# The last block's output tiles stored in two transfers of 64 rows each, three of the eight issued by ScalarE, under another instruction order

## The chip, the cores and the metric

The kernel runs on one core of one Trainium2 chip. The metric is the device time of one execution in microseconds (us). Three runs of the kernel before gave 1031.87, 1032.00 and 1032.98 us, a median of 1032.0 us.

## The reference

The program computes an attention with random features and feeds its output to a two-layer network with a softplus between the layers. What is computed, cut to the core:

```python
q_s, k_s = q / D**0.25, k / D**0.25              # batch 8, heads 8, seq 576, head_dim 64
def phi(x):                                      # 128 features
    h = x @ omega.T - sum(x * x) / 2
    return exp(h - max(h)) / sqrt(128)
kv, z = phi(k_s).T @ v, sum(phi(k_s))            # per batch and head
x = (phi(q_s) @ kv) / (phi(q_s) @ z + 1e-6)      # as 4608 tokens x 512
h = x @ w_in                                     # 512 x 2048
g = max(h, 0) + log1p(exp(-abs(h)))
out = g @ w_out                                  # 2048 x 512, all in float32
```

## The kernel before

The 4608 tokens are worked off as nine blocks of 512. Eight blocks hold the first 512 tokens of each batch; the ninth, called the last block here, holds the 64 tokens left over in each of the eight batches. For each block the network runs in 16 steps. A step is layer 1 for 128 of the 2048 hidden columns (12 matmuls into the PSUM tile `h`, lines 933 to 935), the softplus (three ScalarE activations at lines 939, 942 and 945, one VectorE operation at 948), a split of the result `u` into a rounded high part `gh` (line 952) and a rest `gl` (line 956), and layer 2 (12 matmuls into the four accumulators `acc`, lines 962 to 964, three for each 128 tokens). There are two buffers of each of `u`, `gh` and `gl`. Step 15 of block 8 is written (8,15) here, and so in the tile names of an order (`h_8_15`).

The attention work of the following batch is woven between the steps: projections of keys and queries (`ppk`, `ppq`, line 400, or line 425 from the split tiles `spk`, `spq` that lines 414 and 418 make), sums over keys (`kt`, line 564), and the product that gives `x` (`xp`, line 875). It ends at about 830 us; after that only the network of the last blocks is left.

No engine's order is written out by hand. Every piece of work is an object with an engine, an estimated cost, a due time, predecessors and buffers; `in_order` is a list scheduler that walks a modelled clock and takes, among the pieces that could start soonest, the one with the earliest due time. Some hundred constants (due times, `AHEAD`, `PATIENCE`, `GLUE`, `SPREAD`) decide that order, and the order of the DMA issues on SyncE's queue with it. All DMAs are issued by SyncE (SP).

After step 15 of a block, each of its four accumulators (`tt` 0 to 3) is copied to an output tile `o`, left half by VectorE (`left`, line 996) and right half by ScalarE (`right`, line 999), and stored (`store`). For the first eight blocks the store writes 128 consecutive rows of 2 KB (line 1004). In the last block a tile's 128 rows belong to two batches, 64 rows each; the store writes them in one transfer whose output side has the form 2 x 64 x 512 (line 1006).

Of the kernel before, what the change touches and what calls it, by code (L numbers as in the profile page):

```python
# [20 lines left out]
S = 576  # L21
D = 64
# [12 lines left out]
AHEAD = 312.45  # L35
MARGIN = 0.00
START = {"SP": 0.75, "ACT": 1.9, "PE": 4.6}
SLOW = 10.94
FILL = 0.3
DENSE = 12  # L40
PATIENCE = {"PE": 0.00, "DVE": 0.02, "ACT": 0.17, "POOL": 15.27, "SP": 4.12}
LEAN = {"DVE": 0.56, "POOL": 0.00, "ACT": 0.00}
SPREAD = ((0, 10.51), (17, 8.16))
# [4 lines left out]
GLUE = 67.48  # L48
HOLD = 0.09
START_PACE = 5.26  # L50
EARLY_Q = 7.20
# [135 lines left out]
def favor_softplus_kernel(ctx, tc, q0, k0, qx, kx, tx, vv, om, wi, wo, out):  # L187
# [78 lines left out]
    def plan_weights(nm, fc, due):  # L266
# [36 lines left out]
        def low_part(e):  # L303
# [5 lines left out]
            "SP", 1.46, due + 31.61, load, delay=DL, spare=0 if last else 2,  # L309
# [38 lines left out]
    def plan_unit(q, kind, us, due, early, other=None):  # L348
# [115 lines left out]
        def exponent(j):  # L464
# [9 lines left out]
            "SP", dma(size), due + 15.20, load, behind=prev.get("load"),  # L474
# [7 lines left out]
        if q.b < SPLIT["t" if tail else kind]:  # L482
            r = do("DVE", dve(w), due + 10.58, norms, after=[s], behind=prev.get("norms"), take=sm)
            prev["norms"] = r
            p = do(
                "PE", 0.02 + 0.224 * nt, due - 96.65, project, after=[ld], mode="r",
# [5 lines left out]
            for j in range(2):  # L492
                e = do(
                    "DVE", dve(n // 2 * M), due - 36.44, lambda j=j: maxima(j), after=[p, e], give=[(b, "x")] if j and not early else [],
                )
            e = do("DVE", dve(n), due - 37.34, less_norms, after=[e], port=True)
            e = do("DVE", dve(n), due - 45.13, bias, after=[e], port=True)
            for j in range(2):
                give = [(b, ("ppb", j))]
                es.append(do(  # L500
                    "ACT", n // 2 * 0.25, due - 0.03, lambda j=j: exponent(j), after=[e], behind=es[0] if j else None,
                    give=give + ([(b, "sms")] if j else []),
                ))
        else:
            hs, ls, l = [], [], None
            for j in range(2):
                h = do(
                    ("ACT", "DVE"), (act(w) + 0.1, dve(w, 2) + 0.115), due - 4.01, lambda e, j=j: high(e, j), after=[ld], behind=hs[-1] if hs else None,
                    take=[] if j else [("sp", b, "sps")], port=True,
                )  # L510
                hs.append(h)
                l = do(("DVE", "POOL"), (dve(w) + 0.115, pool(w) + 0.2), due - 76.28, lambda e, j=j: low(e, j), after=[h], behind=l, port=True)
                ls.append(l)
            r = do("DVE", dve(w), due + 30.96, norms, after=[s] + ls, behind=prev.get("norms"), take=sm, give=[(b, "x")])
            prev["norms"] = r
            e, p = None, prev.get("product")
            for t in range(nt):
                p = do(
                    "PE", 0.236, due - 9.84, lambda t=t: product(t), after=ls, behind=p, take=[(kind_, b, ("ppb", t))],
                    give=[(b, "sps")] if t == nt - 1 else [],  # L520
                )
                c = do(
                    ("ACT", "DVE"), (act(2 * M, PSUM), dve(2 * M)), due - 86.17, lambda e, t=t: first(e, t), after=[p], behind=e,
                    take=[] if t else phs,
                )
                e = do("DVE", dve(2 * M), due - 13.53, lambda t=t: second(t), after=[c], give=[(b, ("ppb", t))])
            prev["product"] = p
            e = do("DVE", dve(n * M) + 0.07 * (len(to) - 1), due + 196.21, all_maxima, after=[e, r])
            e = do("DVE", dve(n), due - 55.07, less_norms, after=[e], port=True)
            e = do("DVE", dve(n), due - 36.67, bias, after=[e], port=True)  # L530
            es = []
            for t in range(nt):
                es.append(do(
                    "ACT", 0.587, due - 50.02, lambda t=t: exponents(t), after=[e], behind=es[-1] if es else None,
# [11 lines left out]
        for i in range(len(us)):  # L546
            done.append(plan_queries(q, us[i], due + 1.81 * i, b, es, f"{nm}_{i}", 4 * i))
        plan_flip(q, us, due + 48.99 * (len(us) - 1), b, nm, done)

    def plan_keys(q, us, due, b, es, early):  # L550
# [36 lines left out]
        def plan_turn(after, give=[]):  # L587
            old = quads[q.n - 2].nums if q.n >= 2 else []
            t = do("PE", 0.15, due - 81.14, turn, after=[after], take=[(any_, q.slots, "kv")], give=give)
            q.kvl = do(  # L590
                ("ACT", "DVE"), (act(2 * M, PSUM), dve(2 * M)), due + 3.70, turned, after=[t] + old,
# [4 lines left out]
        if early:  # L596
# [16 lines left out]
            def first_scaled():  # L613
# [4 lines left out]
                "PE", 0.97 if u < 4 else 0.5, due + 9.14, outer, after=es + [q.kvm], give=[(b, "x")],  # L618
                take=[("acc", q.slots, "kt")] if u == 0 else [],
            )  # L620
            if u == 4:
                q.kvl = do(
                    "ACT", act(4 * D + 4, PSUM), due - 59.41, first_scaled, after=[q.kvm], give=[(q.slots, "kt")],
# [4 lines left out]
        def add(e):  # L628
# [16 lines left out]
            ("POOL", "DVE"), (k * pool(w), k * dve(w) + 0.2), due - 71.26, add, after=es + [q.sum],  # L645
# [35 lines left out]
        def in_z():  # L681
# [6 lines left out]
        ldv = do("SP", 1.8, due + 66.39, load_v, take=[("v", q.slots, "v")], delay=DL)  # L688
        q.kvm = do(
            "PE", 0.1 + 0.224 * 10, due - 74.27, burst, after=q.es + [ldv, q.sum], take=[(any_, q.slots, "kt")],  # L690
# [3 lines left out]
            "DVE", dve(4 * M), due - 33.63, flip_sums, after=[q.sum], take=[("flip", q.slots, "st"), ("few", q.slots, "few")], port=True,  # L694
        )
        a = do("ACT", act(2 * M, PSUM), due - 46.64, lambda: scaled(2 * M), after=[q.kvm, z], give=[(q.slots, "kt")])
        plan_turn(a, [(q.slots, "s")])
        z = do("DVE", dve(4 * M), due + 5.39, sums, after=[z], give=[(q.slots, "st")])
        z = do("DVE", 0.55, due - 98.77, last_sums, after=[z], port=True)
        r = do("SP", 0.55, due - 30.52, out_z, after=[z], give=[(q.slots, "few")], delay=DL)  # L700
        q.zc = do("SP", 0.73, due + 123.44, in_z, after=[r], take=[("zb", q.slots, "zb")], delay=DL)

    def plan_first(q, u, due, b, es, nm):
# [51 lines left out]
        def x_low():  # L755
# [3 lines left out]
        t = do("PE", 0.13 * n, due - 118.52, turn, after=es, take=[("any", y, "tp")])  # L759
        h = do(("ACT", "DVE"), (act(n * M, PSUM), dve(n * M)), due - 116.63, turned, after=[t], give=[(y, "tp")])  # L760
        a = do(
            "PE", 0.9, due - 165.51, num, after=[h, q.kvl], take=[("any", y, "nb")], behind=q.nums[-1] if q.nums else None,
            give=[(q.slots, "zb")] if u == NU - 1 else [],
        )
        i = do("DVE", 0.285, due - 134.25, invert, after=[a], take=[("dn", y, "dns")], port=True)
        v = do("DVE", dve(4 * D), due - 140.10, divide, after=[i], give=[(y, "nb"), (y, "dns")])
        k = do("PE", 0.28, due - 64.26, back, after=[v], take=[("any", y, "xb")], give=[(b, "x")])
        q.nums.append(a)
        h = do(
            ("DVE", "ACT"), (dve(2 * w), act(2 * w, PSUM)), due + 2.16, x_high, after=[k], take=[("pt", y, "rs")] if u == 4 else [],  # L770
# [5 lines left out]
        l = do("DVE", dve(2 * w), due + 7.12, x_low, after=[h], give=[(y, "xb")])  # L776
# [3 lines left out]
    def plan_queries(q, u, due, bu, es, nm, first):  # L780
# [21 lines left out]
        def divide(e):  # L802
# [4 lines left out]
            "DVE", 1.6 if u < 4 else 1.35, due + 60.18, den, after=es + [q.zc], take=[("dn", b, "dns")],  # L807
            give=[(q.slots, "zb")] if u == NU - 1 else [], port=True,
        )
        d = do("DVE", 0.09, due - 79.51, invert, after=[d])  # L810
        return do(("POOL", "DVE"), (1.0 * f, dve(n * M)), due + 169.04, divide, after=[d], give=[(b, "dns")], port=True)

    def plan_flip(q, us, due, bu, nm, done):
# [25 lines left out]
        def back():  # L839
# [12 lines left out]
            "DVE", dve(n * M), due + 20.79, flip, after=done, give=[(bu, "phs")], take=[("flip", b, "vs")], port=True,  # L852
        )
        o = do("SP", 0.6 * n_out, due + 53.49, away, after=[t], give=[(b, "vs")], delay=DL, take=[("fd" if u < 4 else "ft", b, "ds")])
        h = do(
            "SP", 0.6 * n_in, due + 4.59, back, after=[o], delay=DL, behind=prev.get("turn"),
# [8 lines left out]
    def plan_x(q, due, t0, w, any_, qt):  # L865
# [27 lines left out]
        def x_low(p):  # L893
# [4 lines left out]
            "PE", 0.00342 * w + 0.02, due - 27.71, num, after=qt["works"] + [q.kvl],  # L898
# [24 lines left out]
    def plan_step(i, t0, n, fc, due, acc, box):  # L923
# [50 lines left out]
        s = do("ACT", act(n, PSUM), due - 35.05, magnitude, after=[a], take=[("u", b, "us")])  # L974
        s = do("ACT", act(n), due + 24.62, decay, after=[s])
        s = do("ACT", act(n), due - 82.94, log, after=[s])
        p = do("DVE", dve(n), due - 23.55, plus, after=[s], give=[(b, "hs")])
        h = do(("DVE", "ACT"), (dve(n, 2), act(n)), due + 23.89, high, after=[p], take=[("g", b, "gs")], port=True)
        l = do(("DVE", "POOL"), (dve(n), pool(n)), due + 31.26, low, after=[h], give=[(b, "us")], port=True)
        box["l1"], ends = a, []  # L980
        for tt in range(n // P):
            e = do(
                "PE", 0.692, due + 10.38, lambda tt=tt: layer2(tt), after=[l, done_w["o", fc]], behind=box.get("l2"),
# [7 lines left out]
        for tt in range(n // P):  # L991
# [9 lines left out]
            def store(tt=tt, o=o):  # L1001
# [216 lines left out]
```

## Time and profile before

| | us |
|---|---|
| median of the runs | 1032.0 |
| the profiled execution's own time | 1030.81 |
| its span, first to last instruction | 1029.0 |
| TensorE busy in the span | 990.7 (96%) |
| mean granted TensorE clock | 0.987 of full speed |

Busy time is the time in which an engine has an instruction of the program at work. The span is what the trace covers; the 1.8 us between it and the execution's own time lie around it. A time such as 1004.03 is counted from the first instruction of the span.

### The profile page before, as it was taken

Reading aid. Unit: us, or ns where it says so; the run is one execution under the profiler, and the core shown is the slowest. Engines: PE = TensorE matmul, PEld = TensorE weight load, DVE = VectorE, ACT = ScalarE, POOL = GpSimd, SP = SyncE. Lnnn points to the kernel's source line nnn. Section 1 sums busy time; section 2 is a strip of 40 time slices with the busy share of each in tenths; the row PEclk is TensorE's granted clock in tenths of the full one; section 3 lists DMA queues with packets and bytes.
Section 4 is the critical chain, followed back from the end, with each engine's and each line's share of the span. In section 5 each row is a group of like instructions: output and inputs, shape, how many; then the busy total and the mean of one; then the engine's idle time right before and its main releaser. Section 6 shows DMA issues by size and latency. Waiting matters only on the chain.

```text
span 1029.0 us, 16459 instructions
## 1 busy us (share of the span) xinstructions
PE 990.7 (96%) x5436; PEld 791.2 (77%) x5436; DVE 713.0 (69%) x1860; ACT 684.5 (67%) x1638; POOL 240.3 (23%) x235
## 2 busy tenths in 40 slices
PE   9999998999999999999999999999999999999990
PEld 8777676787878777777787878878777788888880
DVE  7999998878777877788688868787788342222220
ACT  6999885867676767776786668676767454444440
POOL 2143442242323232322321322323223000000000
PEclk9999998999999999999999999999999999999996
DMA  9874345433333333433434243334331210001001
GB/s 349 312 275 158 123 129 165 138 101 121 113 117 101 130 110 88 134 103 90 132 113 146 75 131 132 126 96 124 118 89 55 83 62 1 1 1 40 1 1 41
DMA packets 64445, 113.78 MB, mean 111 GB/s; under 512 B 18536, under 2 KB 37096, under 8 KB 64360
## 3 DMA queue, kind: packets, MB, share of 16 engines
q1 hardware_dynamic: 64360, 112.73, 34.0%
q8 instruction: 43, 0.70, 0.3%
q14 instruction: 42, 0.34, 0.1%
HBM read 85.68 MB, written 27.03 MB: 110 GB/s over the span
## 4 chain that ended last, share of the span: by engine, by line
PE 76%; DVE 10%; ACT 5%; DMA 4%; issue 2%; POOL 0%; SPq 0%; DVEq 0%; ACTq 0%
PE acc L962 11%; PE h L933 11%; PE h L934 11%; PE h L935 11%; PE acc L963 11%; PE acc L964 11%; PE kt L564 3%; PE ppk L400 3%; PE xp L875 2%; PE ppq L425 2%; DVE junk L795 2%; DMA xq<-q 1%; DMA xq<-qx 1%; DVE flq L826 1%; DVE u L948 1%
## 5 line engine op out<-in xcount | busy, mean ns | idle before, releaser
L962 PE MATMUL acc<-wo,gh 128*128 128x512 f32 x576 | 231.4, 402 | 4.4 <-ACT gh L952 4.4
L933 PE MATMUL h<-xh,wi 128*128 128x512 f32 x576 | 228.2, 396 | 0.0
L963 PE MATMUL acc<-wo,gh 128*128 128x512 f32 x576 | 225.7, 392 | 0.0
L964 PE MATMUL acc<-wo,gl 128*128 128x512 f32 x576 | 225.4, 391 | 0.0
L934 PE MATMUL h<-xl,wi 128*128 128x512 f32 x576 | 224.9, 390 | 0.0
L935 PE MATMUL h<-xh,wi 128*128 128x512 f32 x576 | 224.4, 390 | 0.0
L939 ACT ACTIVATE u<-h 128x512 f32<-128x512 f32 x144 | 86.2, 599 | 173.6 <-PE h L935 148.9
L948 DVE SCALAR_TENSOR_TENSOR u<-h,u 128x512 f32<-128x512 f32 x144 | 98.2, 682 | 134.1 <-ACT u L945 133.0
L962 PEld LDWEIGHTS acc<-wo,gh 128*128 128x128 f32 x576 | 108.4, 188 | 36.9 <-issue 7.7
L933 PEld LDWEIGHTS h<-xh,wi 128*128 128x128 f32 x576 | 108.1, 188 | 26.6 <-issue 3.5
L964 PEld LDWEIGHTS acc<-wo,gl 128*128 128x128 f32 x576 | 108.4, 188 | 24.5 <-DVE gl L956 0.7
L935 PEld LDWEIGHTS h<-xh,wi 128*128 128x128 f32 x576 | 108.1, 188 | 23.2
L934 PEld LDWEIGHTS h<-xl,wi 128*128 128x128 f32 x576 | 108.3, 188 | 20.3
L963 PEld LDWEIGHTS acc<-wo,gh 128*128 128x128 f32 x576 | 108.6, 189 | 19.0
L956 POOL TENSOR_TENSOR gl<-u,gh 128x512 fp32r<-128x512 f32 x51 | 66.4, 1302 | 231.6 <-ACT gh L952 185.6
L952 ACT CAST gh<-u 128x512 fp32r<-128x512 f32 x121 | 75.1, 621 | 53.7 <-PE acc L963 45.5
L795 DVE CUSTOM_DVE_ANT_0 junk<-phq,zb 128x128 bf16<-128x128 f32 (+1 forms) x228 | 82.0, 360 | 16.9 <-DVE dnq L795 0.8
L942 ACT ACTIVATE u<-u 128x512 f32<-128x512 f32 x144 | 91.4, 635 | 3.3
L945 ACT ACTIVATE u<-u 128x512 f32<-128x512 f32 x144 | 91.2, 633 | 3.6
L956 DVE TENSOR_TENSOR gl<-u,gh 128x512 fp32r<-128x512 f32 x93 | 66.6, 716 | 25.6 <-ACT gh L952 24.0
L804 POOL TENSOR_TENSOR phq<-phq,dnq 128x512 f32<-128x512 f32 (+1 forms) x57 | 64.0, 1136 | 54.7 <-DVE dnq L800 35.3
L447 ACT ACTIVATE phq<-phq,smq 128x128 f32<-128x128 f32 x194 | 62.1, 396 | 6.6 <-DVE smq L462 6.5
(125 smaller groups left out, 1370.1 us busy)
## 6 DMA issues: line engine op xcount, KB each, us to landing
xk<-kx SPq DMA_DIRECT2D x28, 512.0 KB, 3.8
xq<-qx SPq DMA_DIRECT2D x28, 512.0 KB, 3.6
fdq<-flq SPq DMA_DIRECT2D x28, 512.0 KB, 2.6
qq<-fdq SPq DMA_DIRECT2D x112, 128.0 KB, 2.9
out<-o SPq DMA_DIRECT2D x36, 256.0 KB, 2.2
rawi<-wi SPq DMA_DIRECT2D x16, 512.0 KB, 7.5
rawo<-wo SPq DMA_DIRECT2D x16, 512.0 KB, 7.9
v<-vv SPq DMA_DIRECT2D x14, 576.0 KB, 4.5
```

What stands on the lines that cost most here:

```text
L795: nc.vector.tensor_tensor_reduce(jk[r, c % jk.shape[1]], ph[r, c], q.zb[r, h], 1.0, 1e-6, ALU.mult, ALU.add, dn[r, 0, c : c + 1])
L933: nc.tensor.matmul(b["h"], wh, xh[:, cc, t], start=cc == 0, stop=False)
L934: nc.tensor.matmul(b["h"], wh, xl[:, cc, t], start=False, stop=False)
L935: nc.tensor.matmul(b["h"], wl, xh[:, cc, t], start=False, stop=cc == NCC - 1)
L939: nc.scalar.activation(b["u"], b["h"], AF.Abs)
L942: nc.scalar.activation(b["u"], b["u"], AF.Exp, scale=-1.0)
L945: nc.scalar.activation(b["u"], b["u"], AF.Ln, bias=1.0)
L948: nc.vector.scalar_tensor_tensor(b["u"], b["h"], 0.0, b["u"], ALU.max, ALU.add)
L956: (nc.vector if e == "DVE" else nc.gpsimd).tensor_tensor(b["gl"], b["u"], b["gh"].bitcast(F32), ALU.subtract)
L962: nc.tensor.matmul(acc[tt], gh, w2[fc][:, 0], start=fc == 0, stop=False)
L963: nc.tensor.matmul(acc[tt], gh, w2[fc][:, 1], start=False, stop=False)
L964: nc.tensor.matmul(acc[tt], gl, w2[fc][:, 0], start=False, stop=fc == NFC - 1)
```

## The change

In the last block each store becomes two transfers of 64 rows by 512 columns, one for each batch. SyncE issues the first half of every tile and the second half of tile 0; ScalarE issues the second half of tiles 1, 2 and 3. Beside that about 80 constants of the scheduler have other values.

```diff
-AHEAD = 312.45
+AHEAD = 322.16
-GLUE = 67.48
+GLUE = 242.04
...
                 if b < B:
                     nc.sync.dma_start(out[b * S + u * P : b * S + (u + 1) * P, :], o["t"])
                     return
-                nc.sync.dma_start(out.rearrange("(b s) d -> b s d", s=S)[2 * u : 2 * u + 2, S - D :, :], o["t"])
+                for j in range(2):
+                    e = nc.scalar if tt and j else nc.sync
+                    e.dma_start(out[(2 * u + j + 1) * S - D : (2 * u + j + 1) * S, :], o["t"][j * D : (j + 1) * D])
```

The first place is the end of the program. On SP, where `o_8_0` to `o_8_3` are the four tiles of the last block and `o_7_3` the last of the block ahead of it, the kernel before has:

```order
L1004 DMA out<-o_7_3_9758 128x512
L1006 DMA out<-o_8_0_10230 2x64x512
L1006 DMA out<-o_8_1_10237 2x64x512
L1006 DMA out<-o_8_2_10244 2x64x512
L1006 DMA out<-o_8_3_10248 2x64x512
```

And the kernel after, on SP:

```order
L1004 DMA out<-o_7_3_9741 128x512
L1008 DMA out<-o_8_0_10231 64x512 x2
L1008 DMA out<-o_8_1_10239 64x512
L1008 DMA out<-o_8_2_10247 64x512
L1008 DMA out<-o_8_3_10252 64x512
```

On ScalarE the program before ends with the split of step (8,15) and four copies:

```order
L952 CAST gh_8_15_10211<-u_8_15_10178 128x512
L999 COPY o_8_0_10230<-acc_8_0_9761 128x256
L999 COPY o_8_1_10237<-acc_8_1_9768 128x256
L999 COPY o_8_2_10244<-acc_8_2_9774 128x256
L999 COPY o_8_3_10248<-acc_8_3_9779 128x256
```

In the kernel after, ScalarE's last rows are:

```order
L952 CAST gh_8_15_10212<-u_8_15_10195 128x512
L999 COPY o_8_0_10231<-acc_8_0_9744 128x256
L999 COPY o_8_1_10239<-acc_8_1_9751 128x256
L1008 DMA out<-o_8_1_10239 64x512
L999 COPY o_8_2_10247<-acc_8_2_9757 128x256
L1008 DMA out<-o_8_2_10247 64x512
L999 COPY o_8_3_10252<-acc_8_3_9762 128x256
L1008 DMA out<-o_8_3_10252 64x512
```

Five of the eight issues stand on SP, and three stand between and behind ScalarE's last copies.

The second place is on VectorE in block 1, where `spq_2_0_2` is the split query tile that the projection `ppq_2_0_2` reads. Before:

```order
L800 RECIPROCAL dnq_2_0_0_1_2351<-dnq_2_0_0_1_2351 128x4
L418 TENSOR_TENSOR spq_2_0_2_2369<-xq_2_0_2_2313,spq_2_0_2_2369 64x512 x2
L956 TENSOR_TENSOR gl_1_0_2389<-u_1_0_2315,gh_1_0_2385 128x512
L390 TENSOR_REDUCE smq_2_0_2_2398<-xq_2_0_2_2313 128x8
L948 SCALAR_TENSOR_TENSOR u_1_1_2380<-h_1_1_2321,u_1_1_2380 128x512
```

After, on VectorE:

```order
L956 TENSOR_TENSOR gl_1_0_2366<-u_1_0_2316,gh_1_0_2351 128x512
L800 RECIPROCAL dnq_2_0_0_0_2346<-dnq_2_0_0_0_2346 128x4
L948 SCALAR_TENSOR_TENSOR u_1_1_2361<-h_1_1_2318,u_1_1_2361 128x512
L414 CAST spq_2_0_2_2391<-xq_2_0_2_2331 64x512 x2
L418 TENSOR_TENSOR spq_2_0_2_2391<-xq_2_0_2_2331,spq_2_0_2_2391 64x512
L637 TENSOR_TENSOR s_2_1_2185<-s_2_1_2185,phk_2_1_2_0_2377 128x512 x2
L418 TENSOR_TENSOR spq_2_0_2_2391<-xq_2_0_2_2331,spq_2_0_2_2391 64x512
```

The rest `gl_1_0` moved ahead of the split tile. On TensorE the projection stands before layer 2 of step (1,0), right behind layer 1 of step (1,2):

```order
L934 MATMUL h_1_2_2362<-xl_81,wi2_548 128x512
L935 MATMUL h_1_2_2362<-xh_80,wi2_548 128x512
L425 MATMUL ppq_2_0_2_0_2391<-omr_87,spq_2_0_2_2369 128x256 x2
L425 MATMUL ppq_2_0_2_1_2394<-omr_87,spq_2_0_2_2369 128x256 x2
L962 MATMUL acc_1_0_2401<-wo0_532,gh_1_0_2385 128x512
```

After, on TensorE, layer 2 of step (1,0) and layer 1 of step (1,3) have gone ahead of it:

```order
L934 MATMUL h_1_3_2414<-xl_81,wi3_710 128x512
L935 MATMUL h_1_3_2414<-xh_80,wi3_710 128x512
L425 MATMUL ppq_2_0_2_0_2437<-omr_87,spq_2_0_2_2391 128x256 x2
L425 MATMUL ppq_2_0_2_1_2440<-omr_87,spq_2_0_2_2391 128x256 x2
L962 MATMUL acc_1_0_2383<-wo1_707,gh_1_1_2412 128x512
```

The projection moved back by 24 matmuls.

The third place is the distance between a step's two layers on TensorE, which is seen best behind the very last layer 1, `h_8_15`. Before, layer 2 of step (8,12) follows it, so three whole layer 2 lie between layer 1 and layer 2 of step (8,15):

```order
L933 MATMUL h_8_15_10158<-xh_80,wi15_2152 128x512
L934 MATMUL h_8_15_10158<-xl_81,wi15_2152 128x512
L935 MATMUL h_8_15_10158<-xh_80,wi15_2152 128x512
L962 MATMUL acc_8_0_9761<-wo12_1763,gh_8_12_10131 128x512
L963 MATMUL acc_8_0_9761<-wo12_1763,gh_8_12_10131 128x512
```

After, it is layer 2 of step (8,13):

```order
L933 MATMUL h_8_15_10175<-xh_80,wi15_2146 128x512
L934 MATMUL h_8_15_10175<-xl_81,wi15_2146 128x512
L935 MATMUL h_8_15_10175<-xh_80,wi15_2146 128x512
L962 MATMUL acc_8_0_9744<-wo13_1856,gh_8_13_10148 128x512
L963 MATMUL acc_8_0_9744<-wo13_1856,gh_8_13_10148 128x512
```

Layer 1 runs one step less ahead of layer 2; so it does in blocks 2 to 7 too.

## Rows read from the trace of the kernel before

**Rows 1.** The page: span; busy us by engine (share of the span) and instructions.
```profile
span 1029.0 us, 16459 instructions
...
PE 990.7 (96%) x5436; PEld 791.2 (77%) x5436; DVE 713.0 (69%) x1860; ACT 684.5 (67%) x1638; POOL 240.3 (23%) x235
```
**Rows 2.** Stretches: length, busy us by engine (instructions), granted clock, DMA share, GB/s.
```profile
150.00:200.00 50.00, 44.09 (x243) 33.24 (x242) 42.51 (x109) 35.65 (x92) 14.36 (x15) 0.93 0.50 150
200.00:250.00 50.00, 50.00 (x285) 39.59 (x284) 38.77 (x105) 36.85 (x93) 17.27 (x16) 1.00 0.38 111
...
950.00:1000.00 50.00, 50.00 (x222) 41.41 (x221) 12.46 (x18) 22.83 (x37) 0.00 (x0) 1.00 0.00 1
1000.00:1029.00 29.00, 5.17 (x23) 3.94 (x21) 2.39 (x5) 1.66 (x5) 0.00 (x0) 0.67 0.10 36
```
**Rows 3.** TensorE's waits over the span: us in total, times, longest.
```profile
PE acc L962 <- ACT gh L952: 4.4, 1, 4.4
PE kt L564 <- DVE xl L895: 2.4, 1, 2.4
```
**Rows 4.** Timeline of the end: start, us, engine, operation [idle before <- releaser].
```profile
1004.03 10.23 SPq L1006 DMA_DIRECT2D out<-o  x4
...
1004.79 0.39 PE L964 MATMUL acc<-wo,gl 128*128 128x512 f32 x1
1005.05 0.37 ACT L999 COPY o<-acc 128x256 f32<-128x256 f32 x1 [0.36 <-DVE o L996]
1005.21 0.42 DVE L996 COPY o<-acc 128x256 f32<-128x256 f32 x1 [0.26 <-PE acc L964]
1005.67 0.37 ACT L999 COPY o<-acc 128x256 f32<-128x256 f32 x1 [0.25 <-DVE o L996]
```
**Rows 5.** Two stretches behind the last copy, columns as in rows 2.
```profile
1008.00:1026.00 18.00, 0.00 (x0) 0.00 (x0) 0.00 (x0) 0.00 (x0) 0.00 (x0) 0.55 0.13 51
1027.00:1028.00 1.00, 0.00 (x0) 0.00 (x0) 0.00 (x0) 0.00 (x0) 0.00 (x0) 0.50 0.02 6
```
**Rows 6.** Waits of SP's queue from 1000 us on: us in total, times, longest.
```profile
SPq L1214 <- DMA out<-o: 13.3, 1, 13.3
```
**Rows 7.** The output's transfers: issue ns min/median/max, first to last start; landing.
```profile
L1004 SPq DMA_DIRECT2D out<-o x32: 332/332/380, 182.8 to 929.2; - x32
L1006 SPq DMA_DIRECT2D out<-o x4: 511/588/8196, 1004.0 to 1006.1; - x4
...
DMA to landing us min/median/max: 2.0/2.2/3.4
```
**Rows 8.** A stretch in which stores of block 7 run, columns as in rows 2.
```profile
926.00:926.50 0.50, 0.50 (x4) 0.42 (x3) 0.40 (x1) 0.39 (x1) 0.00 (x0) 1.00 0.97 369
```
**Rows 9.** Transfers from 64 partitions, `fdq<-flq` of line 837: issue; then issue to landing.
```profile
L837 SPq DMA_DIRECT2D fdq<-flq x28: 513/600/621, 126.6 to 804.5; - x28
...
fdq<-flq SPq DMA_DIRECT2D x28, 64.0 KB, 2.5
```
**Rows 10.** A stretch in which two transfers of line 837 move, columns as in rows 2.
```profile
548.50:549.00 0.50, 0.50 (x14) 0.48 (x10) 0.47 (x2) 0.00 (x0) 0.00 (x0) 1.00 0.76 124
```
**Rows 11.** Timeline of block 1, columns as in rows 4.
```profile
190.34 2.13 DVE L418 TENSOR_TENSOR spq<-xq,spq 64x512 fp32r<-64x512 f32 x2
192.51 0.69 DVE L956 TENSOR_TENSOR gl<-u,gh 128x512 fp32r<-128x512 f32 x1
...
192.53 0.62 PE L425 MATMUL ppq<-omr,spq 128*128 128x256 f32 x3 [0.95 <-DVE spq L418]
```
**Rows 12.** Timeline of the softplus of step (8,15), columns as in rows 4.
```profile
994.33 0.60 ACT L939 ACTIVATE u<-h 128x512 f32<-128x512 f32 x1 [2.32 <-PE h L935]
...
996.29 0.69 DVE L948 SCALAR_TENSOR_TENSOR u<-h,u 128x512 f32<-128x512 f32 x1 [3.56 <-ACT u L945]
...
999.55 0.62 ACT L952 CAST gh<-u 128x512 fp32r<-128x512 f32 x1 [2.10 <-PE acc L963]
...
1000.20 0.69 DVE L956 TENSOR_TENSOR gl<-u,gh 128x512 fp32r<-128x512 f32 x1 [2.03 <-ACT gh L952]
...
1002.29 0.39 PE L962 MATMUL acc<-wo,gh 128*128 128x512 f32 x1
```

More of the change, by code (lines that the diff above doesn't have):

```diff
@@ L47 @@
 UW = 512
-GLUE = 67.48
-HOLD = 0.09
-START_PACE = 5.26
-EARLY_Q = 7.20
+GLUE = 242.04
+HOLD = 0.14
+START_PACE = 5.45
+EARLY_Q = 1.99
 EARLY_T = 0.00
@@ L308, in plan_weights @@
         l = do(
-            "SP", 1.46, due + 31.61, load, delay=DL, spare=0 if last else 2,
+            "SP", 1.46, due + 32.95, load, delay=DL, spare=0 if last else 2,
             take=[({"i": "qh", "o": "ql"}[nm] if last else "w", box, "raw")],
@@ L493, in plan_unit @@
                 e = do(
-                    "DVE", dve(n // 2 * M), due - 36.44, lambda j=j: maxima(j), after=[p, e], give=[(b, "x")] if j and not early else [],
+                    "DVE", dve(n // 2 * M), due - 45.63, lambda j=j: maxima(j), after=[p, e], give=[(b, "x")] if j and not early else [],
                 )
-            e = do("DVE", dve(n), due - 37.34, less_norms, after=[e], port=True)
-            e = do("DVE", dve(n), due - 45.13, bias, after=[e], port=True)
+            e = do("DVE", dve(n), due - 56.40, less_norms, after=[e], port=True)
+            e = do("DVE", dve(n), due - 68.75, bias, after=[e], port=True)
             for j in range(2):
@@ L500, in plan_unit @@
                 es.append(do(
-                    "ACT", n // 2 * 0.25, due - 0.03, lambda j=j: exponent(j), after=[e], behind=es[0] if j else None,
+                    "ACT", n // 2 * 0.25, due + 2.05, lambda j=j: exponent(j), after=[e], behind=es[0] if j else None,
                     give=give + ([(b, "sms")] if j else []),
@@ L518, in plan_unit @@
                 p = do(
-                    "PE", 0.236, due - 9.84, lambda t=t: product(t), after=ls, behind=p, take=[(kind_, b, ("ppb", t))],
+                    "PE", 0.236, due - 16.90, lambda t=t: product(t), after=ls, behind=p, take=[(kind_, b, ("ppb", t))],
                     give=[(b, "sps")] if t == nt - 1 else [],
@@ L533, in plan_unit @@
                 es.append(do(
-                    "ACT", 0.587, due - 50.02, lambda t=t: exponents(t), after=[e], behind=es[-1] if es else None,
+                    "ACT", 0.587, due - 59.22, lambda t=t: exponents(t), after=[e], behind=es[-1] if es else None,
                     give=[(b, "sms")] if t == nt - 1 else [],
@@ L617, in plan_keys @@
             q.kvm = do(
-                "PE", 0.97 if u < 4 else 0.5, due + 9.14, outer, after=es + [q.kvm], give=[(b, "x")],
+                "PE", 0.97 if u < 4 else 0.5, due - 23.80, outer, after=es + [q.kvm], give=[(b, "x")],
                 take=[("acc", q.slots, "kt")] if u == 0 else [],
@@ L686, in in_z @@
             )
-        ldv = do("SP", 1.8, due + 66.39, load_v, take=[("v", q.slots, "v")], delay=DL)
+        ldv = do("SP", 1.8, due + 84.83, load_v, take=[("v", q.slots, "v")], delay=DL)
         q.kvm = do(
-            "PE", 0.1 + 0.224 * 10, due - 74.27, burst, after=q.es + [ldv, q.sum], take=[(any_, q.slots, "kt")],
+            "PE", 0.1 + 0.224 * 10, due - 84.74, burst, after=q.es + [ldv, q.sum], take=[(any_, q.slots, "kt")],
             give=[(x, "phs") for _, x in q.units] + [(q.slots, "v")], mode="c",
@@ L775, in plan_first @@
             return
-        l = do("DVE", dve(2 * w), due + 7.12, x_low, after=[h], give=[(y, "xb")])
+        l = do("DVE", dve(2 * w), due - 8.62, x_low, after=[h], give=[(y, "xb")])
         for p in range(2):
@@ L851, in plan_flip @@
         t = do(
-            "DVE", dve(n * M), due + 20.79, flip, after=done, give=[(bu, "phs")], take=[("flip", b, "vs")], port=True,
+            "DVE", dve(n * M), due + 11.96, flip, after=done, give=[(bu, "phs")], take=[("flip", b, "vs")], port=True,
         )
-        o = do("SP", 0.6 * n_out, due + 53.49, away, after=[t], give=[(b, "vs")], delay=DL, take=[("fd" if u < 4 else "ft", b, "ds")])
+        o = do("SP", 0.6 * n_out, due + 100.27, away, after=[t], give=[(b, "vs")], delay=DL, take=[("fd" if u < 4 else "ft", b, "ds")])
         h = do(
-            "SP", 0.6 * n_in, due + 4.59, back, after=[o], delay=DL, behind=prev.get("turn"),
+            "SP", 0.6 * n_in, due + 21.34, back, after=[o], delay=DL, behind=prev.get("turn"),
             take=[] if qt["works"] else [("q", qt, "tag")], give=[(b, "ds")],
@@ L1005, in store @@
                     return
-                nc.sync.dma_start(out.rearrange("(b s) d -> b s d", s=S)[2 * u : 2 * u + 2, S - D :, :], o["t"])
-            a = do("DVE", 0.34, due - 2.24, left, after=[ends[tt]], take=[("end" if last else "t2", o, "s")])
-            r = do("ACT", 0.27, due - 105.06, right, after=[ends[tt]] if last else [a], behind=a if last else None, give=[(box, ("acc", i, tt))])
-            do("SP", 0.75, due - 38.80, store, after=[a, r], give=[(o, "s")], delay=2.0)
+                for j in range(2):
+                    e = nc.scalar if tt and j else nc.sync
+                    e.dma_start(out[(2 * u + j + 1) * S - D : (2 * u + j + 1) * S, :], o["t"][j * D : (j + 1) * D])
+            a = do("DVE", 0.34, due - 67.36, left, after=[ends[tt]], take=[("end" if last else "t2", o, "s")])
+            r = do("ACT", 0.27, due - 124.99, right, after=[ends[tt]] if last else [a], behind=a if last else None, give=[(box, ("acc", i, tt))])
+            do("SP", 0.75, due - 64.17, store, after=[a, r], give=[(o, "s")], delay=2.0)
     def plan_rest(due):
```

108 lines of the change are left out of this document (54 added, 54 removed).

## The prediction, as put on record before the run

> **What bounds the kernel now.** I read the page first: TensorE is busy for 990.7 of 1029.0 us [rows 1], so what can be gained without less arithmetic is 38.3 us at most. The table by stretches says where these lie. From 200 to 250 us TensorE works without a gap, and so it does from 950 to 1000; from 150 to 200 it is idle for 5.9 us at a granted clock of 0.93; and from 1000 us on it works 5.17 of 29.0 us [rows 2]. This end holds 29.0 - 5.17 = 23.8 us of the idle time, and everything ahead of it 38.3 - 23.8 = 14.5 us. Of the 14.5, the list of waits names 4.4 us before a layer 2 and 2.4 us before the key sums [rows 3].
>
> The timeline of the end shows what the 23.8 us are. The last matmul starts at 1004.79; VectorE copies the left half of the last tile from 1005.21, ScalarE the right half from 1005.67 to 1006.04 [rows 4]. No engine computes after that, and 23 us remain. SP issues four stores from 1004.03 to 1014.26 [rows 4]; the last issue alone takes 8.2 us, where a store of the earlier blocks takes 0.33 [rows 7]. Then SP waits another 13.3 us for the output's transfer [rows 6], until 1027.5, and the rest, 1.5 us, is the program's closing. The DMA engines move only 51 GB/s from 1008 to 1026, at a busy share of 0.13 [rows 5], which is 2 of 16 engines, and next to nothing from 1027 on. Four stores of 256 KB are 1.05 MB, and at 51 GB/s this takes 21 us: so from soon after the first issue until 1027.5 the end is bound by two DMA engines and by nothing else. A store of 128 consecutive rows moves at 369 GB/s and a share of 0.97 [rows 8] and lands 2.2 us after its issue begins (2.0 to 3.4) [rows 7]. That view's landing times can't hold the four last stores, since the last alone took from 1006.1 to 1027.5.
>
> **The change part by part.** *The form of the stores.* The old output side is 2 x 64 x 512, with two things in its outermost place, and two engines were busy; the rows of one batch are 64 x 512. Whether 64 rows reach more than two engines is read from the transfers out of 64 partitions in line 837: two of 64 KB each, in pieces far smaller than 2 KB, hold the engines busy at a share of 0.76, or 12 of 16, while little else moves [rows 10], and they land 2.5 us after their issue [rows 9]. I therefore take the landing of a 64-row half as that of an earlier block's store, 2.2 us, with 2.0 and 3.4 as its bounds [rows 7]. Eight halves carry the same bytes; a tile comes every 0.62 us (ScalarE's copies start at 1005.05 and 1005.67 [rows 4]), and 256 KB at 369 GB/s [rows 8] need 0.71 us, so a backlog of some 0.3 us may form over four tiles, which is inside the bounds.
>
> *The issues.* SP issues five halves. At 0.33 us each [rows 7] it is free when the last copy ends, so the first half of tile 3 is issued at about 1006.07. The issues on ScalarE are the one thing that no row shows: none of its DMAs is in the trace. Each stands ahead of the next tile's right copy, so its length counts. From below it is nothing, for then the copies stay where they are; from above I take 0.62 us, the longest issue of 64 partitions on SP [rows 9]. At 0.62 the issue after tile 1's copy delays the copies of tile 2 by 0.3 and that of tile 3 by 0.6 in all, and the last issue ends at about 1007.3. The nearest row is SP's 0.33 for a plain store, which fits between two copies 0.25 us apart with a delay of about 0.1 us for each; behind the last copy the second half of tile 3 is then issued at about 1006.2. I take 1006.1 for both halves.
>
> *The end.* 1006.1 + 2.2 + 1.5 of closing = 1009.8 for the span, 19.2 us less than 1029.0. With 2.0 us of landing it is 1009.6; with 3.4 us and the slow issues it is 1006.7 + 3.4 + 1.5 = 1011.6. So this part gives 17.4 to 19.4 us.
>
> *The order.* It carries the same matmuls, one dummy matmul more, so the order can only change the idle time of 14.5 us and the half clock behind it (0.07 of 50 us, 3.5 us, in the stretch at 150 us [rows 2]). From below that is 18.0 us gained. From above it is unbounded by any row; I take as much again lost, 18.0. Two places can be read. In block 1 TensorE waited 0.95 us for the split query tile, which VectorE finished at 192.47 [rows 11]. Now 24 matmuls go first, layer 2 of step (1,0) and layer 1 of (1,3): at 0.227 us each (the 222 matmuls of a full stretch of 50 us [rows 2] give 0.225) 5.4 us, while VectorE's part comes later by one `gl`, one `u` and a cast pair, and one sum between its halves, some 3 us together (0.69 for `gl` [rows 11], the same for `u` [rows 12], the rest about as the 2.13 us pair [rows 11] is long). The wait should go: -0.95. The wait of 4.4 us before layer 2 [rows 3] stays where it was for all that the order shows, since the same VectorE work still stands ahead of the `gl` that this layer 2 needs. Nothing else can be read off, and the stretches from 200 us on were full already. Of the ends -18.0 and +18.0 I take -0.95, near to the full stretches.
>
> *The sum.* 1030.81 (the profiled execution's own time) - 19.2 - 0.95 = 1010.7. The median of the runs lies 1.2 us above that execution, and I carry this over: 1011.9 us.
>
> A rule of the skill speaks against the change. The Trainium skill, DMA: Bandwidth & Descriptors, section "Rules for kernel authors", says of two transfers to disjoint partition halves: "Don't bother", since both spread over all 16 engines and take turns there, and that issuing from several engines saves issue time alone. By it nothing changes, and the time stays at 1030.8. The same page, section "Why a DMA increments its semaphore by 16 and not by 1", has the count of engines as the largest number up to 16 that divides the slowest dimension on both sides: 2 for the old form, 16 for 64 rows. The trace's 0.13 agrees with the second and takes away the first's premise, that the single transfer already uses 16 engines.
>
> **The rivals.** *The halves don't help.* If a 64-row half also runs on two engines, or the halves queue behind one another, 1.05 MB still take 21 us and the time is 1031 to 1032. For it: no store of 64 rows by 2 KB is in the trace. Against it: rows 10.
>
> *The order gives more.* If the waits of 4.4 and 2.4 us go [rows 3] and with the first the half clock (3.5), 1011.9 - 10.3 = 1001.6. For it: these sit in blocks 0 and 1, where the order is denser than elsewhere. Against: the sequence on TensorE and VectorE around both is nearly what it was.
>
> *The shorter lead makes TensorE wait.* Layer 1 now runs one step less ahead of layer 2. Behind the last step that is harmless, and the trace says why: its `u` is ready at 996.98, 2.85 us after the first matmul behind layer 1 would start (994.1), yet the split waits until 999.55 for a buffer that layer 2 of (8,13) frees, and `gl` is ready 1.4 us before layer 2 needs it [rows 12]; now that layer 2 comes first, split and rest end 4.2 us behind layer 1, with 24 matmuls or 5.4 us to cover them. In blocks 1 to 6, though, attention work stands between these operations on ScalarE and VectorE. If the cover fails there once in each block as it did in block 0, at 4.4 us a time [rows 3], six times, 26.4 us are lost: 1038.3, slower than before. It decides from 20.2 us of waits on, about 0.2 us for each of these 96 steps. A smaller case, one to three such waits or slow issues on ScalarE, gives 1015 to 1028. Against it: the wait for the buffer in rows 12 shows that the longer lead was spent waiting.
>
> **How the numbers follow.** Forecast, 1008.5 to 1015: 0.60. Order gives more, 1000 to 1008.5: 0.20. Smaller losses, 1015 to 1028: 0.12. Halves don't help: 0.04. Slower: 0.04. A measurement of this kernel tells 0.2%, about 2 us, from no change. Faster therefore has 0.60 + 0.20 + 0.12 = 0.92, same 0.04, slower 0.04. The range from 1005 to 1018 leaves out about half of the second case and two thirds of the third with the last two, some 0.2 in all.
>
> **What the changed profile would show.** Right: the DMA share behind the last copy near 0.9 for 2 to 3 us in place of 0.13 for 21; SP's last issue well under 1 us; SP's final wait about 2 us; TensorE's idle time at the end about 4.6 us in place of 23.8; the wait for the split tile in block 1 gone. Wrong would be: a share of 0.13 again; ScalarE's last copies spaced by more than 0.7 us; waits of layer 2 for `gh` or `gl` in blocks 2 to 7, or a full stretch after 200 us that is no longer full.

## The result and the profile after

The kernel after takes 1022.81 us (median of four runs, 1020.95 to 1024.72), the kernel before in the same session 1031.93 us (1031.37 to 1032.98). The ratio is 0.9911, with a 95% interval from 0.9889 to 0.9932: faster by 9.1 us. The forecast was 1011.9 us with a range from 1005 to 1018, so the sign was right and the size was less than half of what was forecast.

The first lines of the page after, to be read against [rows 1]:

```profile
span 1021.6 us, 16368 instructions
PE 996.1 (98%) x5438; PEld 794.3 (78%) x5438; DVE 730.4 (72%) x1905; ACT 675.2 (66%) x1601; POOL 224.4 (22%) x227
```

TensorE's idle time fell from 38.3 to 25.5 us, but its busy time rose by 5.4. Next the timeline of the end (columns as in [rows 4]; `SPq` and `ACTq` are DMA issues by SP and ScalarE):

```profile
1014.88 3.21 SPq L1008 DMA_DIRECT2D out<-o  x5
...
1015.56 0.55 ACTq L1008 DMA_DIRECT2D out<-o  x1
...
1016.20 0.37 ACT L999 COPY o<-acc 128x256 f32<-128x256 f32 x1 [0.67 <-DVE o L996]
1016.61 0.49 ACTq L1008 DMA_DIRECT2D out<-o  x1
1017.14 0.37 ACT L999 COPY o<-acc 128x256 f32<-128x256 f32 x1 [0.56 <-ACT o L999]
1017.54 0.50 ACTq L1008 DMA_DIRECT2D out<-o  x1
```

The stretches of the end (columns as in [rows 2]), the issues of line 1008 with their landing, and SP's last wait:

```profile
1016.00:1017.00 1.00, 0.02 (x1) 0.00 (x0) 0.42 (x1) 0.37 (x1) 0.00 (x0) 1.00 0.89 197
1017.00:1018.00 1.00, 0.00 (x0) 0.00 (x0) 0.00 (x0) 0.37 (x1) 0.00 (x0) 1.00 1.00 188
1018.00:1019.00 1.00, 0.00 (x0) 0.00 (x0) 0.00 (x0) 0.00 (x0) 0.00 (x0) 1.00 1.00 352
1019.00:1020.00 1.00, 0.00 (x0) 0.00 (x0) 0.00 (x0) 0.00 (x0) 0.00 (x0) 0.61 0.85 287
```

```profile
L1008 SPq DMA_DIRECT2D out<-o x5: 511/556/607, 1014.9 to 1017.5; - x5
...
L1008 ACTq DMA_DIRECT2D out<-o x3: 488/498/547, 1015.6 to 1017.5; - x3
...
DMA to landing us min/median/max: 2.3/2.9/3.2
```

```profile
SPq L1216 <- DMA out<-o: 2.3, 4, 0.9
```

The DMA share behind the last copies is 0.85 to 1.00 where it was 0.13 [rows 5], and SP's wait is 2.3 us where it was 13.3 [rows 6]. The span ends 5.6 us behind the last matmul's end (1016.02), where it ended 23.8 us behind: the new stores gave 18.2 us at the end. But that last matmul ends 10.8 us later than before (1016.02 against 1005.18). The list of TensorE's waits says where to look (columns as in [rows 3]):

```profile
PE ppq L425 <- DVE spq L418: 3.9, 7, 1.2
PE acc L964 <- DVE gl L956: 3.7, 1, 3.7
PE ppk L400 <- DMA xk<-kx: 3.5, 5, 1.2
PE kt L564 <- DVE xl L895: 2.4, 1, 2.4
PE acc L962 <- ACT gh L952: 1.4, 1, 1.4
```

The 4.4 us for `gh` has split into 1.4 and 3.7. From 200 us on the first and the third line are new: a projection of queries that waits for its split tile (seven times, 3.9 us), and one of keys that waits for the load of `xk` (two of the five times, 2.4 us; the other three lie before 200 us, where the kernel before waits for such a load too, 0.3 us). All but one of these nine waits lie between 350 and 650 us, where TensorE was idle for 0.6 us in all before and is idle for 6.8 us now. First the kernel before, then the kernel after (columns as in [rows 2]):

```profile
450.00:500.00 50.00, 50.00 (x279) 39.66 (x276) 39.35 (x105) 35.80 (x90) 15.08 (x14) 1.00 0.34 100
```

```profile
450.00:500.00 50.00, 47.48 (x267) 36.89 (x266) 40.33 (x107) 33.11 (x84) 14.64 (x14) 1.00 0.33 104
500.00:550.00 50.00, 49.79 (x271) 39.47 (x273) 41.56 (x111) 32.34 (x80) 13.45 (x14) 0.97 0.33 102
```

What both waits have in common is a load on SP's queue. SP's part of the timeline shows the place at quad (4,0), the first half of batch 4's heads. There `zd` is the store of its sums over keys to DRAM and `zb` the load that reads them back into all 128 partitions. Before:

```profile
435.28 0.35 SPq L377 DMA_DIRECT2D xq<-qx  x1
437.62 0.31 SPq L679 DMA_DIRECT2D zd<-few  x1
...
442.76 1.38 SPq L377 DMA_DIRECT2D xk<-kx  x1
...
444.67 0.42 SPq L683 DMA_DIRECT2D zb<-zd  x1
450.46 0.33 SPq L377 DMA_DIRECT2D xq<-qx  x1
```

After:

```profile
433.46 0.38 SPq L679 DMA_DIRECT2D zd<-few  x1
436.85 0.33 SPq L683 DMA_DIRECT2D zb<-zd  x1
437.34 0.33 SPq L377 DMA_DIRECT2D xq<-qx  x1
437.73 0.42 SPq L833 DMA_DIRECT2D fdq<-flq  x1
445.84 1.76 SPq L849 DMA_DIRECT2D qq<-fdq  x4
447.71 0.58 SPq L377 DMA_DIRECT2D xk<-kx  x1
```

Before, seven microseconds and two loads lie between `zd` and `zb`, and six more before the next `xq`. After, `zb` stands right behind `zd`: SP stands still from 433.9 to 436.8 until `zd` has landed, and `xq` and the store `fdq` are issued behind the broadcast. The same shows over the whole trace in SP's waits for a `zd` at the head of its queue (columns as in [rows 6]), before and after:

```profile
SPq L683 <- DMA zd<-few: 4.9, 2, 2.5
```

```profile
SPq L683 <- DMA zd<-few: 20.6, 10, 3.4
```

SP's waits from 437 to 447 us in the kernel after, and the wait that follows on TensorE:

```profile
SPq L849 <- DMA fdq<-flq: 7.6, 1, 7.6
SPq L683 <- DMA zd<-few: 2.9, 1, 2.9
```

```profile
452.30 0.94 PE L400 MATMUL ppk<-omf,xk 64*128 64x128 f32 x12 [1.18 <-DMA xk<-kx]
```

And the DMA engines while the broadcast moves:

```profile
438.00:439.00 1.00, 1.00 (x6) 0.82 (x5) 0.45 (x2) 1.00 (x5) 0.00 (x0) 1.00 1.05 119
439.00:440.00 1.00, 1.00 (x8) 0.79 (x6) 0.67 (x1) 1.00 (x5) 0.00 (x0) 1.00 0.92 59
```

They are full at 59 to 119 GB/s, where plain stores moved 369 [rows 8]. `fdq` lands 8.1 us after its issue, `qq`, which reads it back, holds SP until then, and `xk` is queued behind `qq`. That gave three suspects for the experiments: the store code, the wait at the head of SP's queue, and the broadcast in front of `xq`.

### The profile page after: what moved, and what is told of

Its sections match the earlier page's. It is cut to its first block, busy times and chain, and to the rows that moved or that the text cites. A ratio compares the mean times of both kernels' runs of the same rounds, so it can differ in the third digit from the quotient of the medians.

```text
span 1021.6 us, 16368 instructions
## 1 busy us (share of the span) xinstructions
PE 996.1 (98%) x5438; PEld 794.3 (78%) x5438; DVE 730.4 (72%) x1905; ACT 675.2 (66%) x1601; POOL 224.4 (22%) x227
## 4 chain that ended last, share of the span: by engine, by line
PE 69%; DVE 14%; DMA 9%; ACT 4%; issue 2%; SPq 0%; ACTq 0%; POOL 0%; DVEq 0%; POOLq 0%
PE h L933 10%; PE acc L962 10%; PE h L934 10%; PE h L935 10%; PE acc L964 10%; PE acc L963 10%; DMA fdq<-flq 3%; DMA xk<-kx 3%; PE kt L564 3%; DVE junk L795 3%; PE xp L875 2%; PE ppq L425 2%; PE ppk L400 2%; DMA xq<-q 1%; DVE u L948 1%
## 5 line engine op out<-in xcount | busy, mean ns | idle before, releaser
L963 PEld LDWEIGHTS acc<-wo,gh 128*128 128x128 f32 x576 | 108.6, 189 | 18.9
L795 DVE CUSTOM_DVE_ANT_0 junk<-phq,zb 128x128 bf16<-128x128 f32 (+1 forms) x228 | 92.0, 404 | 22.3 <-ACT phq L447 7.2
L956 DVE TENSOR_TENSOR gl<-u,gh 128x512 fp32r<-128x512 f32 x100 | 71.3, 713 | 33.4 <-ACT gh L952 30.8
L956 POOL TENSOR_TENSOR gl<-u,gh 128x512 fp32r<-128x512 f32 x44 | 57.3, 1301 | 152.1 <-ACT gh L952 119.4
L804 POOL TENSOR_TENSOR phq<-phq,dnq 128x512 f32<-128x512 f32 (+1 forms) x57 | 60.2, 1061 | 130.0 <-DVE dnq L800 112.6
L470 ACT ACTIVATE phk<-ppk,smk 128x128 f32<-128x128 f32 x230 | 62.9, 383 | 16.6 <-DVE smk L462 14.3
```

The costliest lines, as they stand in the source:

```text
L795: nc.vector.tensor_tensor_reduce(jk[r, c % jk.shape[1]], ph[r, c], q.zb[r, h], 1.0, 1e-6, ALU.mult, ALU.add, dn[r, 0, c : c + 1])
L956: (nc.vector if e == "DVE" else nc.gpsimd).tensor_tensor(b["gl"], b["u"], b["gh"].bitcast(F32), ALU.subtract)
L963: nc.tensor.matmul(acc[tt], gh, w2[fc][:, 1], start=False, stop=False)
```

## The experiments

**The two parts apart, and the store without ScalarE.** The first run is the kernel before with the new store, the second the kernel after with the old store, that is with this edit reversed.

```diff
-                nc.sync.dma_start(out.rearrange(...)[2 * u : 2 * u + 2, S - D :, :], o["t"])
+                for j in range(2):
+                    e = nc.scalar if tt and j else nc.sync
+                    e.dma_start(out[(2 * u + j + 1) * S - D : (2 * u + j + 1) * S, :], o["t"][j * D : (j + 1) * D])
```

> The new stores under the order of the kernel before, nothing else. Theory A, the stores give 18.2 us (23.8 us of the end become 5.5, as in the changed kernel's trace) and the new order takes about 9 to 11 us back: 1013 to 1015 us, TensorE's last matmul ends near 1005 us as before. Theory B, the new stores themselves bring most of the loss (another queue, other waits all through the program) and the order is neutral: 1021 to 1024 us as in the changed kernel, with the last matmul near 1016 us.

Measured: 1015.45 us (1014.98 to 1016.63), ratio 0.9837 [0.9822, 0.9852], 16.7 us less than the kernel before beside it (1032.19). That is theory A, half a microsecond past its range; the last matmul ends at 1008.21, not near 1005.

> The new order with the old stores, nothing else. Theory A: slower than the kernel before by what the order costs, 1041 us (1039 to 1043), DMA share 0.13 behind the last copy for some 21 us. Theory B: 1031 to 1033 us, as before.

Measured: 1038.17 us (1037.87 to 1042.62), ratio 1.0068 [1.0042, 1.0095]. That is theory A too, 0.8 us short of its range. The order alone costs 6.0 us (4.3 to 9.8 by the interval); put on top of the new store it costs 1022.81 - 1015.45 = 7.4. Two lines of TensorE's waits under the order alone:

```profile
PE ppq L425 <- DVE spq L418: 5.0, 8, 1.6
...
PE ppk L400 <- DMA xk<-kx: 3.3, 4, 1.3
```

Of the second line, 0.9 us lies behind 200 us; with the stores alone neither wait occurs there. So the store is a gain, the order a loss, the two add up within the interval (-16.7 + 6.0 = -10.7, where both together gave -9.1), and the new waits come with the order.

The third run is the first with all eight halves on SP.

```diff
-                    e = nc.scalar if tt and j else nc.sync
-                    e.dma_start(out[...], o["t"][j * D : (j + 1) * D])
+                    nc.sync.dma_start(out[...], o["t"][j * D : (j + 1) * D])
```

> The new stores under the order of the kernel before, with all eight halves issued by SyncE. If ScalarE's issues (0.49 to 0.55 us each, standing between its copies) cost the 0.6 us by which the last copies came late, but eight issues of 0.55 us on one queue take 4.4 us from the first: SyncE's last issue begins about 4 us after its first instead of 2.7, so the end is 0.5 to 1.5 us longer than in the run with the stores alone: 1014 to 1016 us. If the issues on SyncE were only 0.33 us each as for 128 rows: 0.3 us shorter instead.

Measured: 1015.01 us (1014.89 to 1016.05), ratio 0.9833 [0.9819, 0.9848], the same as with ScalarE's three. Its end:

```profile
1005.36 5.00 SPq L1008 DMA_DIRECT2D out<-o  x8
...
1007.00 0.37 ACT L999 COPY o<-acc 128x256 f32<-128x256 f32 x1 [0.25 <-DVE o L996]
```

The copies are on time again (1007.00, half a microsecond behind the last matmul's end at 1006.51), but eight issues take SP 5.0 us, and the span ends 6.6 us behind the last matmul where it is 5.6 with ScalarE's help. That is 1.0 us in the trace of the end and nothing that the medians can tell.

**`zb` behind the load.** In the kernel after, the `zb` loads of the seven quads (4,0) to (7,0) are put behind the next `xq` load and `fdq` store on SP. The relative order on all other engines stays. (Line numbers are 18 higher here and in the runs built on this one.) In the edit, `sp` holds the next two pieces of work on SP, and nothing moves unless they are a load and a store.

```diff
+    for z in [w for w in out if name(w) == "in_z"][6:13]:
...
+        out.insert(sp[1] + 1, z)
+        del out[i]
```

> The changed kernel with one SyncE step in another place: the seven transfers zb<-zd of quads (4,0) to (7,0), which the new order issues straight ahead of an xq load and an fdq store, are issued straight behind these two. The order of all other engines is unchanged. Theory C, this broadcast holds the DMA engines at about 1.0 of busy share while moving 59 to 119 GB/s, so that the xq load and the fdq store behind it land 6 and 8 us after their issue and TensorE waits for ppk and ppq in blocks 3 to 6: the waits of 1.2 us on xk<-kx and on spq there go, the xq loads land in about 4 us, and the time falls by 5 to 9 us to 1014 to 1018. Theory D, the waits come from the shorter lead of layer 1 and from VectorE's order: they stay, and the time stays within 2 us of the changed kernel's 1022.8.

Measured: 1011.38 us (1009.95 to 1013.79), ratio 0.9798 [0.9778, 0.9818]: 11.4 us less than the kernel after, more than theory C gave, and less than the new store alone. The same place on SP, and two of the stretches:

```profile
433.36 0.38 SPq L697 DMA_DIRECT2D zd<-few  x1
435.68 0.33 SPq L395 DMA_DIRECT2D xq<-qx  x1
436.10 0.39 SPq L851 DMA_DIRECT2D fdq<-flq  x1
436.72 0.33 SPq L701 DMA_DIRECT2D zb<-zd  x1
441.00 2.38 SPq L867 DMA_DIRECT2D qq<-fdq  x4
445.12 0.35 SPq L395 DMA_DIRECT2D xk<-kx  x1
```

```profile
450.00:500.00 50.00, 50.00 (x284) 39.89 (x285) 42.46 (x114) 35.04 (x89) 14.49 (x14) 1.00 0.35 106
500.00:550.00 50.00, 50.00 (x281) 39.47 (x280) 41.97 (x112) 33.13 (x84) 14.45 (x15) 1.00 0.37 119
```

`xk` is issued 2.6 us earlier, and the stretches are full. So the loss of the order sits in these seven transfers. Whether the wait in the queue or the broadcast does it, this run can't tell, since both moved.

**The wait without the broadcast, and the broadcast without the wait.** The first of the two is the run with `zb` late and, at each of `zb`'s seven old places, a DMA of 2 KB that reads `zd`:

```diff
+        t = dram.tile([16, 32], F32, ...)
+        nc.sync.dma_start(t, q.zd)
```

> As the run with the broadcast zb moved back behind the xq load and the fdq store (1011.4 us), but at the seven old places of zb stands a DMA of 2 KB that reads zd and goes to an unused tile in DRAM; it brings back the wait for zd's landing at the head of SP's queue, without the broadcast. Theory A (the wait at the queue's head is what costs, 2.3 to 2.9 us per place): the xq load and the fdq store are issued 2 to 3 us later again, the waits of ppq for spq and ppk for xk come back to at least two thirds, 1018 to 1022 us. Theory B (the broadcast's occupation of the DMA engines is what costs): issues come later but land 3.9 and 2.9 us behind their issue, TensorE's waits stay as in the run with zb late, 1011 to 1014 us. If both add: 1014 to 1018 us.

Measured: 1013.55 us (1012.9 to 1014.91), ratio 0.9824 [0.981, 0.9837].

The second is the kernel after, where `zb` of these quads reads other data, for which it need not wait, so that the denominators of these quads are left out (line numbers behind the edit are one higher):

```diff
+            z = (om if 8 <= q.n < 15 else q.zd).rearrange("a b -> (a b)")[: 4 * M]
...
-                q.zd.rearrange("a b -> (a b)").unsqueeze(0).broadcast_to([P, 4 * M]),
+                z.unsqueeze(0).broadcast_to([P, 4 * M]),
```

> The kernel after, with the seven broadcasts zb of quads (4,0) to (7,0) at their places, but reading 512 numbers of omega, which have been in DRAM since the start, in place of zd, so the denominators of those quads are left out; the wait for zd at the head of SP's queue is gone and the 256 KB of broadcast remain. Theory A (the wait costs): waits of ppq for spq and ppk for xk mostly gone, 1011 to 1015 us. Theory B (the broadcast costs): xq still lands 5 to 6 us and fdq 7 to 8 us behind its issue, waits remain, 1018 to 1022 us. Both add: 1015 to 1018 us.

Measured: 1011.62 us (1010.91 to 1012.65), ratio 0.9804 [0.979, 0.9817].

Both theories fell: without the broadcast the time came out as if the broadcast were the cost, without the wait as if the wait were. The wait alone brings back some 2 of the 11.4 us, the broadcast alone 0.2, and their sum is far from the whole. The rows of SP's waits around 437 to 447 us suggest why. With the broadcast alone:

```profile
SPq L850 <- DMA fdq<-flq: 5.8, 1, 5.8
SPq L377 <- DVE smq L390: 0.9, 1, 0.9
```

SP still waits 0.9 us for VectorE to free the buffer of the next `xk` (1.7 us with `zb` late). A delay smaller than that is swallowed there. With the wait alone this wait is down to nothing, and in the kernel after the delay is past it.

**Two waits, no broadcast.** That reading can be tested: if lateness is all that counts, more of it without any broadcast must bring the loss back.

```diff
         nc.sync.dma_start(t, q.zd)
+        t2 = dram.tile([16, 32], F32, ...)
+        nc.sync.dma_start(t2, t)
```

> As the run with the wait alone (1013.6 us), but behind the DMA of 2 KB stands a second one that reads what the first wrote, so SP's queue stands still for about 1.9 us more at each of the seven places, still without a broadcast. From the traces at 433 us: counted from the issue of v, the xk load of the next unit lands at +16.0 with zb late, +16.1 with the broadcast alone, +16.7 with the wait alone and +19.1 in the kernel after; with the broadcast alone SP then still waits 0.9 us for a free buffer, with the wait alone 0.03. Theory C (only lateness counts: each place has about 2 us that SP spends waiting anyway, and every delay past that, from whatever cause, goes to TensorE): xk lands at about +18.6, the waits of ppk for xk and of ppq for spq come back, and the time is 1018 to 1022 us, near the kernel after. Theory D (it takes the broadcast itself, at work in the same moments as the xq load): no such return, 1014 to 1016 us.

Measured: 1027.34 us (1024.77 to 1029.87), ratio 0.9954 [0.9939, 0.9968]: past the range that was given for lateness, and far from the other. The waits of TensorE from 200 to 830 us:

```profile
PE ppq L443 <- DVE spq L436: 7.1, 11, 2.1
```

Set in order of lateness, the five runs of the new order agree. The two columns of landings count from the issue of `zd` and are means over the seven quads, each landing read from SP's transfers. The waits are TensorE's for `spq` and `xk` from 200 to 830 us, added up from its list. The kernel before, which ran beside each of them, had medians from 1031.9 to 1032.2.

| run | `xq` lands | `xk` lands | waits, us | median, us |
|---|---|---|---|---|
| `zb` late | 5.4 | 16.3 | 0.2 | 1011.4 |
| broadcast alone | 7.1 | 17.1 | 0.6 | 1011.6 |
| wait alone | 7.4 | 17.5 | 1.3 | 1013.6 |
| kernel after | 8.5 | 18.9 | 6.3 | 1022.8 |
| two waits | 9.4 | 19.4 | 8.0 | 1027.3 |

As long as `xk` lands by 17.1 us, nothing is lost that the medians can tell; at 17.5 it is 2 us. From 17.5 to 18.9, 1.4 us in each of seven places or 9.8 us in all, the time grows by 9.3: past the slack the delay goes to the end about one for one. The last step, 0.5 us in each place and 3.5 in all, costs 4.5. By the landings of `xq`, whose split tile most of the waits are for, the two steps are 7.7 and 6.3 us in all against the same 9.3 and 4.5, so the order of the runs is firm and the price of a microsecond rough. In the kernel after TensorE's waits make up about half of the loss; the other half is busy time (below).

**The rule for every quad.** The same move for every `zb` behind which a load and a store follow, by which one more is moved, in block 1.

```diff
-    for z in [w for w in out if name(w) == "in_z"][6:13]:
+    for z in [w for w in out if name(w) == "in_z"]:
```

> The rule that moves zb behind the following load and store on SP, applied to all quads; by the order it moves eight of them, one more than before (quad (1,1), in block 1). Theory (zb ahead of a load is what costs, wherever TensorE has no work stored): the same 1011 us or up to 1 us less, for that quad had no wait behind it in the kernel after; both kernels are beaten by 10 and 20 us. Rival (the seven moves only happened to fall well, any other order differs by a few us either way): outside 1009 to 1013 us.

Measured: 1011.59 us (1011.11 to 1011.78), ratio 0.9802 [0.9789, 0.9816]. It can't be told from the run with seven moved. Both versions beat the kernel before by 20 and the kernel after by 11 us.

## Why the prediction was wrong, and where it was right

**The order, the step that failed.** The prediction took -0.95 us; measured is +6.0 (order alone) to +7.4 (on the new store), so 6.9 to 8.3 us of the 10.9 us by which the forecast was short. The place that was read came out as read: the wait of 0.95 us for the split query tile in block 1 [rows 11] is gone. Yet up to 200 us TensorE is idle for 12.9 us in the kernel after and for 12.5 in the kernel before, so this term isn't shown to have been worth anything. What failed is the sentence "Nothing else can be read off, and the stretches from 200 us on were full already". SP's order can be read off as well, and there `zb` had moved from behind two loads to right behind its `zd`. The sign that the prediction gave for such a loss, a full stretch after 200 us that is no longer full, is there. And a full stretch says that nothing is lost at present, not how much later a load may come: the bound above was open for that reason, and -0.95 was taken from the wrong end. The order is not bad as a whole. With the seven transfers put right it is 4.1 us better than the old one (1011.38 against 1015.45). Two lines of TensorE's waits in the run with the stores alone, which the run with `zb` late does not have, hold 2.0 us of that; they lie between 200 and 830 us:

```profile
PE ppq L425 <- DVE phq L438: 1.3, 4, 0.6
...
PE kt L564 <- DVE phq L438: 0.7, 1, 0.7
```

The rest was not located. Of the 10.6 us of span between the kernel after and the run with `zb` late, 5.6 is idle time of TensorE and 5.0 busy time. The waits at 499 to 500 us were followed by a stretch of 3.4 us at half the clock (granted 0.50, that is 1.2 GHz; the 0.97 from 500 to 550 us above, 1.00 with `zb` late), which is 1.7 of the 5.0; where the other 3.3 sit stays open. Such a stretch doesn't follow every wait: under the order alone TensorE waited 1.65 us up to 497.4 us, and the granted clock stayed at 1.00 from 450 to 550.

**The stores, mis-sized by a little.** The mechanism held: a half of 64 rows fills the DMA engines (0.85 to 1.00 against 0.13 [rows 5]), and the rival that the halves don't help fell. The rule quoted in the prediction from the Trainium skill, DMA: Bandwidth & Descriptors, section "Rules for kernel authors" (don't bother with two transfers to partition halves), did not hold where the single transfer used 2 engines of 16 (the share of 0.13). The term was 19.2 us; the end gave 18.2. Of its pieces, the issues were taken at 0.33 us [rows 7] and take 0.50 to 0.56 in the median, nearer to the upper bound from line 837 [rows 9]. On ScalarE they delay the last copies, which start 1.04 and 0.94 us apart (more than 0.7, one of the prediction's own signs of being wrong), so the last issue stands 1.5 us behind the last matmul's end (1017.54 against 1016.02) where 0.9 was taken (1006.1 against 1005.18). The landing is 3.2 us where 2.2 was taken, and the likely cause is that the last halves queue behind the others (share 1.00 at 1017 and 1018 us): with all halves on SP, issued over 5.0 us, they land after 2.3 to 2.5 us. The closing is 0.8 instead of 1.5. Together 0.6 + 1.0 - 0.7 = 0.9. In medians the store alone gave 16.7, another 1.5 us less. That lies ahead of the end: the last matmul ends at 1008.21 with the stores alone, 3.0 us later than before (1005.18), and at 1006.51 with all halves on SP, though nothing was changed there. The profiled execution before was a quick one, 1.4 us under the median beside that run (1030.81 against 1032.19), and that of the stores alone lies 0.2 us above its own, so 3.0 - 1.4 - 0.2 = 1.4 remain of it in the medians. The 1.2 us that the forecast carried from the profiled execution to the median thus came from one execution and did not carry over. One part of the later matmuls is a stretch of 3.4 us at half the clock at 111 us, behind the wait of 2.4 us for `xl` [rows 3], which TensorE has in those executions and not in that of before. The profiled execution of the kernel after has it as well, worth 1.7 of the 10.8 us by which its last matmul came later. Why it comes in one execution and not in another is not settled.

**The shorter lead.** The rival by which layer 1 in blocks 1 to 6 makes TensorE wait fell: the list of waits has only one for `gh` and one large one for `gl`, both in block 0. Its smaller neighbour, "one to three such waits", had the right range, 1015 to 1028, for the wrong mechanism. The wait of 4.4 us in block 0 stayed, as said, in two pieces (1.4 and 3.7). The sum of what the range leaves out was also off: half of 0.20, two thirds of 0.12, and 0.08 are 0.26, not 0.2.

## What to carry to other kernels

A reordered program is read on every queue, the DMA queue first: a transfer that reads what was stored just before it stalls everything behind it (here for 1.0 to 3.0 us at each of seven places), and a load can lose its lead without any change in the order of the computing engines. Before a delay is costed, look for what the queue waits for anyway: up to that slack two delays can be nearly free one by one (2.0 and 0.2 us here) and dear together (11.4). Where the program ends in a transfer, its busy share (0.13 here) shows in one row whether its form is the bound.

## What was not expected of the hardware

- Issuing a store of 64 rows takes longer than one of 128 rows: 0.51 to 0.61 us on SP and 0.49 to 0.55 on ScalarE, against a median of 0.33 [rows 7].
- A load that spreads 2 KB over 128 partitions (256 KB written) holds the DMA engines at a share of 0.92 to 1.05 while they move 59 to 119 GB/s, and the 512 KB load of `xq` issued behind it lands after 5.9 us, where its median over the kernel after is 3.9. The broadcast is not worse in this than a plain transfer of twice its size: with the stores alone, an `xq` issued behind a 512 KB `fdq` lands after 5.4 to 6.0 us.
- A 2 KB transfer from DRAM to DRAM takes 1.8 us from issue to landing in the median. The 2 KB `zd` takes 1.3 to 3.4 us at the seven places of the kernel after; the 3.4 us is where a load of 576 KB was issued 0.4 us ahead of it.
